# A spectral gating kernel on Trainium2: the last six lower-half filter products cut into column halves, and the work list written anew

## The chip, the cores and the metric

The kernel runs on one core of a Trainium2 chip. TensorE (PE) multiplies matrices, VectorE (DVE), ScalarE (ACT) and GpSimd (POOL) work element by element, SyncE (SP) only issues transfers; ACT and POOL issue transfers too. The engines run side by side, each through its own instructions in order, and wait for each other on semaphores. The metric is the device time of one execution in microseconds (us), the median over runs.

## The reference

```python
def _A_ref(x, w_r, w_i):                       # _B_ref is the same
    X = jnp.fft.rfft2(x.astype(jnp.float32), axes=(-2, -1))
    X = X * (w_r + 1j * w_i)
    return jnp.fft.irfft2(X, s=(S, D), axes=(-2, -1)).astype(jnp.bfloat16)

x = A_x                                        # (1, 2048, 1024) bf16
g = sigmoid((x * gate_w).sum(-1, keepdims=True))
return g * _A_ref(x, A_w_r, A_w_i) + (1 - g) * _B_ref(x, B_w_r, B_w_i)
```

Both branches work on the same x. It is transformed once, multiplied by two filters of 2048 x 513 complex numbers, and the two results are mixed row by row with the gate g. One inverse transform does for both, because the gate is folded into its row factors.

## The kernel before

**Stages.** The two-dimensional transform is done as matrix products with constant tables. A job name stands for one step on one piece of data:

- `load.x.g.dh`: one of 16 loads of x, 256 KB each: row group g (0 to 7), column half dh. `load.E`, `load.F2`, `load.CK` are tables. `egen` makes signed copies of E.
- `fold.g.k` and `s1m.g.j`, `s1e.g.j`: the first row transform. For a group in `FOLDED` (0, 1, 2 before) DVE makes the sum and the difference of columns d and 1023-d (two `tensor_tensor`, L456), and PE then needs 16 matmuls of 128 columns in a group. For the others DVE makes one reversed copy (L454), and PE does the fold itself with 16 matmuls of 256 columns. `s1e` takes the result out of PSUM.
- `s2m`, `s2e`: the column transform. `s4m`, `s4e`: the second row transform. Both run for p = 0 to 7 and for two column halves of the spectrum: h = 1 (upper) first, then h = 0 (lower).
- `swap.p.h` (two transfers within SBUF) and `xneg.p.h` (a sign) make the copy with real and imaginary parts exchanged.
- `prod.t.h`, t = 0 to 15: the filter products for both filters, one DVE `tensor_tensor` of 128x2048 at L317, both inputs in SBUF. Filters are loaded by `load.W.h.b.m.f`: h, the first block b of four t's, m blocks, filter f (A or B). Four slots hold them: three in tile WR, the fourth in tile FR. `wslot(h, b)` says which; a slot is loaded again only when the products that read it are done. `w5` takes a column of each upper block aside.
- `s5m.g`, `s5e.g`: the inverse second row transform; groups 16 to 31 read h = 1 products, groups 0 to 15 read h = 0 products. Every one of them waits for all 16 products of its half (key `("prod", h)`). `c0m`, `c0e` put the first column right.
- The gate: `gwm`, `gsm.t0.n` (dot products of x with gate_w taken from the transformed rows, n values of t at a time), `gse`, `rowsum`, `zsm`, `zse` (sigmoid), `zst` (store to a DRAM scratch tensor `zd`), `zld` (load it back, spread over the partitions, key `SI`). `stm`, `ste`, `stx`, `stp.k` serve the column 512.
- `rb.c` (POOL or DVE) multiplies a quarter of the inverse row table U5 with the gate, `al.c.k` rearranges it. `s6m`, `s6e`: the inverse first row transform. `s7m`, `s7c`, `s7p`, `fin`: the inverse column transform and its butterflies; `store.i.sg`: the output.

**Order.** The string `ORDER` (L21) lists all jobs. It is read once from left to right; each job appends its instructions to its engine's queue (the last letter of a job: a = ACT, d = DVE, p = POOL, s = SP), and the semaphore waits follow from the keys that the instructions read and write. So the list fixes the order on each engine, and it also fixes who gets which of the four PSUM units: `take` hands out the unit that was given back first. DVE works on the products while ACT takes `s5m` results of the upper half out of PSUM; SP issues the filter loads between them, one after another, and waits at each of them for its slot.

The lines that set when a product may start, and who waits for the products, are these:

```python
wslot = lambda h, b: b if h else b % 3                                   # L362
mult(Q[eng], o, i0, i1, r=K + KS + wkeys(slot, 0) + wkeys(slot, 1) + [("XN", t // 2, h)] + U * h, a=[("prod", h)])   # L544
r=["CK", ("prod", g // 16)] + (["col0"] if g == 0 else [])               # L670, s5m
mult(Q[eng], o, o, sl(F2, 512 * c, [(32, 16), (0, 2), (1, 32)]), r=["U5", "SI"], a=[("RP", c)])                      # L655, rb
```

Of the kernel before, what the change touches and what calls it, by code (L numbers as in the profile page):

```python
# [20 lines left out]
ORDER = """  # L21
load.E.1.s load.x.6.0.s zero load.SM.a load.GR.a egen.1.1 load.x.6.1.s egen.1.2 load.x.3.0.a load.x.0.0.s load.x.3.1.s egen.1.3 load.E.0.s
fold.6.0.d load.x.7.0.s load.x.7.1.s load.x.0.1.s warm.12x64x1.14x512x1 fold.3.0.d s1m.6.1 load.x.4.0.a s1e.6.1.d load.x.4.1.a s1m.6.0
s1m.3.1 fold.7.0.d load.x.1.1.s load.x.1.0.s egen.0.1 sig0 load.x.5.0.s rev s1e.3.1.a fold.0.1.d fold.0.0.d s1m.3.0 s1m.7.1 s1m.7.0
fold.4.0.d load.x.5.1.s s1e.3.0.a load.x.2.1.s s1m.0.0 s1e.7.1.a load.x.2.0.s s1e.6.0.a s1m.0.1 fold.1.1.d s1m.4.0 s1e.7.0.a s1m.4.1
fold.1.0.d s1e.0.1.a s1m.1.0 s1e.0.0.d s1e.4.0.a load.F2.s fold.5.0.d s1m.5.0 s1e.4.1.a s1m.5.1 load.CK.s load.W.1.0.3.1.s s1e.1.0.a
fold.2.0.d load.W.1.0.3.0.s fold.2.1.d s1m.2.1 s1e.5.0.a s1m.1.1 s1e.2.1.a s1e.5.1.d s1m.2.0 s1e.1.1.d s1e.2.0.a s2m.0.1 s2m.1.1 s2e.0.1.a
s2m.5.1 s4m.0.1 s2e.1.1.d s2e.5.1.d s4m.1.1 s2m.2.1 s4e.0.1.a s2m.4.1 s4e.1.1.a s2e.4.1.a s4m.5.1 s2e.2.1.d s2m.3.1 s2m.6.1 swap.0.1.p
s4e.5.1.a swap.1.1.p s2e.6.1.a s2e.3.1.d xneg.0.1.d w5.0.d s2m.7.1 s4m.3.1 s2e.7.1.a load.W.1.3.1.0.s prod.1.1.d swap.5.1.p xneg.1.1.d
s4m.4.1 s4m.2.1 s4m.6.1 prod.0.1.d prod.2.1.d prod.3.1.d s4e.3.1.a s4m.7.1 s4e.4.1.a s4e.2.1.a xneg.5.1.a swap.3.1.s prod.11.1.d swap.4.1.s  # L30
gwm gwe.a s2m.1.0 xneg.3.1.d gsm.12.4 w5.1.a s4e.7.1.a s4e.6.1.a load.VC.s swap.2.1.p gse.12.4.a w5.2.d load.W.1.3.1.1.s xneg.4.1.a gsm.0.4
s2e.1.0.a gse.0.4.a gsm.4.4 xneg.2.1.a swap.7.1.p s2m.0.0 gse.4.4.a s2m.2.0 s2e.0.0.a s2e.2.0.a s2m.5.0 gsm.8.4 prod.7.1.d s2e.5.0.a
prod.9.1.d prod.6.1.d gse.8.4.a prod.10.1.d s4m.1.0 s4m.0.0 s2m.7.0 s4e.1.0.a s2m.3.0 swap.6.1.p s4e.0.0.a xneg.7.1.a prod.8.1.d s2e.7.0.a
xneg.6.1.d prod.4.1.d prod.5.1.d load.W.0.0.1.0.s load.W.0.0.1.1.s s4m.2.0 swap.1.0.p rowsum.0.d prod.14.1.d prod.12.1.d s4e.2.0.a s2m.4.0
s2e.3.0.a s4m.5.0 s2m.6.0 swap.0.0.p stm load.W.0.1.2.1.s prod.15.1.d w5.3.a s4e.5.0.a prod.13.1.d rowsum.1.d load.W.0.1.2.0.s ste.a
xneg.0.0.a s5m.24 stp.2.d prod.0.0.d s4m.7.0 s2e.6.0.a swap.2.0.p s2e.4.0.a xneg.1.0.d swap.5.0.p s4m.3.0 s5e.24.a s4e.3.0.a s5m.19
s4e.7.0.a s5m.27 s5e.27.a rowsum.2.p swap.7.0.p prod.2.0.d s4m.4.0 s5m.29 swap.3.0.p s5m.16 s5e.19.a s4e.4.0.a prod.3.0.d prod.1.0.d s5m.23
xneg.5.0.d s5e.23.a stx.s s4m.6.0 zsm swap.4.0.s s5e.29.a s4e.6.0.a zse load.W.0.3.1.1.s s5m.22 xneg.2.0.d s5m.26 prod.11.0.d s5e.22.a
s5e.26.a prod.5.0.d zst.p s5e.16.a prod.4.0.d xneg.4.0.a load.W.0.3.1.0.s s5m.30 swap.6.0.p s5m.20 s5m.28 s5m.18 xneg.3.0.d s5e.30.a s5m.31
xneg.7.0.a prod.10.0.d s5e.28.a load.U5.s prod.7.0.d prod.6.0.d xneg.6.0.a prod.8.0.d s5m.21 s5e.18.a s5m.17 s5e.21.a s5e.31.a prod.9.0.d  # L40
prod.14.0.d prod.12.0.d s5e.20.a prod.13.0.d s5m.25 zld.s prod.15.0.d s5m.10 s5e.25.a s5m.6 s5m.12 s5e.17.d stp.0.d s5e.10.a s5m.9 s5m.11
s5e.6.d s5m.7 stp.1.d s5e.12.a rb.0.p s5m.8 rb.3.p s5e.9.a s5e.11.d s5e.7.a s5m.13 c0m s5e.8.d s5e.13.a s5m.4 c0e.d s5m.3 s5m.2 s5e.4.a
al.0.0.p s5e.3.d s5m.1 s5e.2.a s5m.14 s5m.5 s5e.1.d al.0.1.p s5e.14.a s5m.0 s5e.0.d rb.2.p s5m.15 rb.1.d s6m.0.1 al.1.1.d s5e.5.a s5e.15.a
s6e.0.1.a s6m.1.1 s6m.0.0 s6e.1.1.d s6e.0.0.a s6m.1.0 s6e.1.0.d al.2.1.p load.DI.s s7m.0 s7m.1 s7c.0.a s7p.0.0.d s7c.1.a s7p.0.1.d s7m.2
al.1.0.p s7p.1.0.d s6m.2.1 al.2.0.a s7c.2.a s6m.2.0 s7p.2.0.d s7p.2.1.d s6e.2.1.a s7p.1.1.d s6e.2.0.a s6m.3.0 fin.0.1.p fin.0.0.p s7m.3
fin.2.0.d s7c.3.a s6e.3.0.a s7m.4 fin.1.1.d s7c.4.a s6m.3.1 fin.1.0.d s7p.3.0.d s7p.3.1.d fin.2.1.p store.0.1.s s7m.5 s6e.3.1.a fin.3.0.p
s7p.4.0.d s6m.4.1 s7m.7 s7p.4.1.d s6m.4.0 fin.4.1.d s7c.5.a al.3.0.a fin.4.0.p s7p.5.0.d s7c.7.a s7p.5.1.d store.0.0.s fin.3.1.d s6m.5.1
al.3.1.a store.1.0.p s6e.4.1.a s7m.6 fin.5.0.d s6e.4.0.a s7p.7.0.d store.1.1.s s7p.7.1.d s7m.8 s7c.6.a s6m.5.0 fin.5.1.p fin.7.1.p s7p.6.0.d
s7c.8.a s7p.6.1.d s6e.5.1.a fin.7.0.d s7p.8.0.d store.5.1.s s6e.5.0.a fin.6.1.p store.4.1.s store.3.1.s s6m.6.1 store.5.0.s s7p.8.1.d
fin.6.0.d s7m.9 s6e.6.1.a s7m.10 store.6.0.s store.7.1.s fin.8.0.d store.3.0.p s7c.10.a s7m.11 s7c.9.a s6m.6.0 s7p.10.0.d s7c.11.a  # L50
store.2.1.a store.2.0.p s7p.10.1.d fin.8.1.p store.4.0.s s7p.9.0.d s7p.9.1.d fin.10.0.p s6m.7.1 fin.9.1.d store.7.0.s s6e.6.0.a s7p.11.0.d
store.8.0.p s6e.7.1.a s6m.7.0 s7p.11.1.d s6e.7.0.a s7m.13 fin.10.1.p s7c.13.a s7m.12 store.10.0.s fin.9.0.d store.8.1.p s7c.12.a store.9.0.s
s7m.14 s7p.13.0.d fin.11.1.p s7m.15 s7p.12.0.d fin.11.0.p s7c.14.a store.10.1.s s7p.13.1.d store.9.1.s s7p.12.1.d fin.13.1.p store.6.1.s
s7p.14.0.d store.11.0.s s7p.14.1.d s7c.15.a s7p.15.0.d store.14.0.a fin.13.0.p store.11.1.s store.14.1.a s7p.15.1.d store.13.1.a
store.15.0.s store.15.1.a fin.12.0.d fin.12.1.d store.12.1.a store.12.0.s store.13.0.p
# [329 lines left out]

# [426 lines left out]
```

## Time and profile before

| | us |
|---|---|
| three runs | 132.91, 132.07, 132.33 |
| median | 132.33 |
| the profiled execution, its own time | 132.75 |
| span of its instructions | 130.9 |
| busy: PE, DVE, ACT, POOL | 106.9, 104.2, 98.2, 51.0 |

The profiled execution took 1.85 us more than the span of its instructions, and it is 0.42 us above the median. Times in the views count from the start of the span. In a row of the timeline stand the start, the duration, engine, line, operation, written tile <- read tile, shapes and a count; rows of one kind that follow each other are merged, so a row with x9 is nine instructions. In brackets stands the idle time before it and what ended it. A row of the windows view has, for a stretch of time, the busy time and number of instructions of each engine, then the granted share of the TensorE clock, the busy share of the DMA engines, and GB/s.

### The profile page before, as it was taken

The page shows a single profiled execution, that of the slowest core. Times are in us where ns is not written, and L with a number is a line of the kernel's source. Part 1 is how long each engine was busy: PE and PEld are TensorE (multiplying, and loading weights), DVE is VectorE, ACT ScalarE, POOL GpSimd, SP SyncE. Part 2 cuts the span into 40 slices and gives each one's busy share as a digit, 9 for nine tenths or more (in the row PEclk, how much of TensorE's full clock was granted, in tenths as well). Part 3 has the DMA queues.
Part 4 walks back from the last instruction along what each step waited for, and adds up shares of the span by engine and source line. Part 5 has one row for each costly group of instructions (what it writes and reads, how often), then busy time and mean ns, then how long its engine had stood idle before and what let it go on. Part 6 is the DMA issues. An engine that isn't in the chain of part 4 may idle for free.

```text
span 130.9 us, 3622 instructions
## 1 busy us (share of the span) xinstructions
PE 106.9 (82%) x1522; PEld 88.5 (68%) x1529; DVE 104.2 (80%) x126; ACT 98.2 (75%) x120; POOL 51.0 (39%) x63
## 2 busy tenths in 40 slices
PE   6966789699999999778775358999999997969920
PEld 3344577588759988546475258999999896959500
DVE  0404795373699998999499999988699999999990
ACT  1913599647799969999999994899568987766410
POOL 3000000007316106332540007990439394949970
...
GB/s 108 253 279 371 348 385 304 201 264 323 290 115 224 292 148 189 252 297 326 267 162 214 250 403 233 5 0 5 0 5 40 80 23 88 103 276 43 203 200 241
DMA packets 27314, 25.55 MB, mean 195 GB/s; under 512 B 2706, under 2 KB 23458, under 8 KB 27042
## 3 DMA queue, kind: packets, MB, share of 16 engines
...
## 4 chain that ended last, share of the span: by engine, by line
PE 50%; ACT 19%; DVE 13%; DMA 6%; issue 5%; SPq 3%; DVEq 1%
PE PS L332 50%; ACT FR L312 9%; ACT WP L312 7%; DMA WP<-in_A_x_dram 6%; DVE FR L729 4%; DVE WP L317 4%; SPq L308 3%; ACT FR L321 2%; DVE WR L735 2%; DVE FR L314 2%; DVEq L751 1%; DVE WR L729 1%; DVE WP L314 0%; ACT XST L312 0%; ACT W L312 0%
## 5 line engine op out<-in xcount | busy, mean ns | idle before, releaser
L312 ACT ACTIVATE WP<-PS 128x1024 bf16<-128x1024 f32 x51 | 50.2, 1035 | 11.9 <-PE PS L332 11.7
L312 ACT ACTIVATE FR<-PS 128x1024 bf16<-128x1024 f32 (+1 forms) x44 | 36.6, 897 | 11.9 <-PE PS L332 11.9
L332 PE MATMUL PS<-FR,WP 128*128 128x128 bf16 (+2 forms) x383 | 32.9, 245 | 2.2 <-DVE FR L729 1.9
L332 PEld LDWEIGHTS PS<-FR,WP 128*128 128x128 bf16 x384 | 28.5, 130 | 6.2 <-DVE FR L729 2.8
L332 PE MATMUL PS<-CK,WP 128*128 128x64 bf16 x512 | 22.5, 209 | 8.5 <-ACT WP L312 4.9
L332 PEld LDWEIGHTS PS<-CK,WP 128*128 128x128 bf16 x512 | 20.9, 121 | 10.5 <-ACT WP L312 5.8
L735 POOL TENSOR_TENSOR WR<-FR 128x512 bf16<-128x512 f32 x15 | 20.3, 1379 | 9.9 <-DVE FR L729 9.8
L314 DVE CAST WP<-PS 128x1024 bf16<-128x1024 f32 (+1 forms) x14 | 16.1, 1166 | 7.3 <-PE PS L332 7.3
L317 DVE TENSOR_TENSOR WP<-FR,WR 128x2048 bf16<-128x2048 bf16 x16 | 18.5, 1220 | 1.8 <-issue 1.8
L332 PE MATMUL PS<-F,FR 128*128 128x128 bf16 x256 | 17.3, 230 | 1.3 <-DVE FR L314 1.3
L308 POOL DMA_DIRECT2D WP<-WP x12 | 6.7, 558 | 29.5 <-ACT WP L312 29.5
L332 PEld LDWEIGHTS PS<-F,FR 128*128 128x128 bf16 x256 | 16.2, 104 | 2.7 <-DVE FR L314 1.4
L729 DVE TENSOR_TENSOR FR<-PS,FR 128x512 f32<-128x512 f32 x28 | 17.5, 679 | 0.4 <-ACT FR L312 0.4
L332 PE MATMUL PS<-WP 128*128 128x256 bf16 (+1 forms) x128 | 12.7, 253 | 3.9 <-DMA WP<-in_A_x_dram 1.8
L332 PEld LDWEIGHTS PS<-WP 128*128 128x128 bf16 x128 | 10.3, 98 | 6.5 <-DMA WP<-in_A_x_dram 2.1
L317 DVE TENSOR_TENSOR WP<-WP,WR 128x2048 bf16<-128x2048 bf16 x12 | 14.0, 1221 | 0.0
L308 POOL DMA_DIRECT2D FR<-FR x14 | 7.9, 569 | 13.8 <-PE PS L332 12.9
L735 DVE TENSOR_TENSOR WR<-FR 128x512 bf16<-128x512 f32 x13 | 12.7, 1010 | 0.1
L317 POOL TENSOR_TENSOR FR<-FR,F 128x1024 bf16<-128x1024 bf16 x3 | 6.4, 2144 | 10.4 <-DMA F<-zd 10.4
L332 PE MATMUL PS<-WP,CK 128*128 128x512 bf16 (+4 forms) x42 | 7.8, 324 | 0.1
L314 DVE COPY WP<-WP 128x1024 bf16<-128x1024 bf16 x5 | 2.1, 423 | 7.2 <-DMA WP<-in_A_x_dram 7.2
L332 PE MATMUL PS<-FR,CK 128*128 128x512 bf16 (+1 forms) x32 | 7.0, 352 | 1.0 <-ACT FR L312 0.8
(51 smaller groups left out, 79.1 us busy)
## 6 DMA issues: line engine op xcount, KB each, us to landing
WP<-in_A_x_dram SPq DMA_DIRECT2D x13, 256.0 KB, 7.8
out_dram<-WR SPq DMA_DIRECT2D x20, 128.0 KB, 2.1
FR<-FR POOLq DMA_DIRECT2D x14, 128.0 KB, 3.1
WP<-WP POOLq DMA_DIRECT2D x12, 128.0 KB, 3.4
...
WP<-in_A_x_dram ACTq DMA_DIRECT2D x3, 256.0 KB, 7.8
out_dram<-WR POOLq DMA_DIRECT2D x6, 128.0 KB, 2.2
```

Source lines behind the costliest of these rows:

```text
L308: return P.add(eng, lambda e: e.dma_start(dst, src), dma=name, **kw)
L312: P.add("act", lambda e: e.activation(dst, src, ACT.Copy), **kw)
L314: P.add(eng, lambda e: e.tensor_copy(dst, src), **kw)
L317: P.add(eng, lambda e: e.tensor_tensor(out=dst, in0=s0, in1=s1, op=ALU.mult), **kw)
L321: P.add("act", lambda e: e.activation(dst, src, ACT.Copy, scale=SM[:, col:col + 1]), **kw)
L332: P.add("pe", lambda e: e.matmul(o, lh, rh, start=first, stop=last), **kw)
L729: P.add(Q[eng], lambda e: e.tensor_tensor(out=o, in0=ps(u * 1024, [(1, 512)]), in1=eos(i), op=ALU.subtract if s else ALU.add), r=[("EO", i ...
L735: P.add(Q[eng], lambda e: e.tensor_tensor(out=od, in0=pv[0], in1=pv[1], op=ALU.subtract if s else ALU.add), r=[("PQ", i % NPQ, 0), ("PQ", ...
L751: with nc.Block() as block:
```

## The change

- `FOLDED` becomes (0, 1, 2, 3): group 3 is folded on DVE as well.
- `HALVED = (5, 6, 7)`: the lower-half products of p = 5, 6, 7 (t = 10 to 15) become two instructions each, for the lower and the upper 32 of 64 column blocks (`prod.t.0.0`, `prod.t.0.1`, 128x1024 each). The key of the lower half is split likewise: `s5m` groups 0 to 7 wait for part 0, groups 8 to 15 for part 1. `s4e` of these p's writes another layout.
- `wslot(1, b)` becomes `(b - 1) % 4`: upper blocks 1, 2, 3 lie in WR and are loaded first, block 0 lies in FR.
- `gsm` runs in eight groups of two t's instead of four groups of four.
- `keep.k.n` is new: n matmuls of 512 columns whose result nobody reads. `keep.3.2` stands ahead of `s2m.3.0`, `keep.1.2` ahead of `s5m.7`, `keep.2.2` and `keep.0.2` behind the last `s7m`.
- The list is new. On the engines' queues: five more loads of x go by ACT and five fewer by SP; three `xneg` and one `s4e` move from ACT to DVE, one `s5e` from DVE to ACT, `rb.1` from DVE to POOL; `c0e` goes to ACT; `stp.1` stands ahead of the lower products with t = 10 and up and `stp.0` between their first and their second halves. `w5` is all on ACT, and one `s1e` and one `s6e` more are on DVE; `al` has two jobs on POOL (four before), four on ACT (three), two on DVE (one); SP issues one swap more and three stores fewer. The upper products run in the order 10 11 4 7 6 5 15 8 1 9 3 0 14 12 13 2, before 1 0 2 3 11 7 9 6 10 8 4 5 14 12 15 13.

```diff
-FOLDED = (0, 1, 2)
+FOLDED = (0, 1, 2, 3)
+HALVED = (5, 6, 7)
...
-    wslot = lambda h, b: b if h else b % 3
+    wslot = lambda h, b: (b - 1) % 4 if h else b % 3
...
+    def keep(k, n):
+        u = take("keep", k)
+        for v in range(n):
+            mm(ps(u * 1024 + 512 * (v % 2), [(1, 512)]), sl(CK, 0, [(1, 128)]), sl(CK, 0, [(1, 512)]), True, True, r=["CK"], w=banks(u)[v % 2:v % 2 + 1])
+        give("keep", k)
...
-    def prod(t, h, eng):
+    def prod(t, h, c, eng):
...
+        nq, q0 = (64, 0) if c == 2 else (32, 32 * c)
...
+        mult(Q[eng], o, i0, i1, r=K + KS + wkeys(slot, 0) + wkeys(slot, 1) + [("XN", t // 2, h)] + U * h,
+             a=[("prod", h, v) for v in range(2) if c in (2, v)])
...
-               r=["CK", ("prod", g // 16)] + (["col0"] if g == 0 else []), w=banks(u)[q // 8:q // 8 + 1])
+               r=["CK", ("prod", g // 16, g % 16 // 8)] + (["col0"] if g == 0 else []), w=banks(u)[q // 8:q // 8 + 1])
```

The part of the two lists that the prediction follows, one engine each, from the end of the upper products on:

```
DVE before  prod.13.1 rowsum.1 stp.2 prod.0.0 xneg.1.0 prod.2.0 prod.3.0 prod.1.0 xneg.5.0 xneg.2.0 prod.11.0 prod.5.0
            prod.4.0 xneg.3.0 prod.10.0 prod.7.0 prod.6.0 prod.8.0 prod.9.0 prod.14.0 prod.12.0 prod.13.0 prod.15.0
            s5e.17 stp.0 s5e.6 stp.1 s5e.11 s5e.8 c0e s5e.3 s5e.1 s5e.0 rb.1 al.1.1 s6e.1.1 s6e.1.0 s7p.0.0
DVE after   prod.13.1 rowsum.0 prod.2.1 rowsum.1 xneg.0.0 xneg.1.0 prod.0.0 xneg.5.0 prod.2.0 prod.3.0 stp.2 stp.1 prod.1.0
            xneg.2.0 prod.11.0.0 prod.4.0 xneg.4.0 prod.10.0.0 prod.5.0 prod.8.0 prod.9.0 xneg.7.0 prod.6.0 prod.15.0.0
            prod.7.0 prod.14.0.0 prod.13.0.0 prod.12.0.0 stp.0 prod.13.0.1 prod.11.0.1 prod.10.0.1 prod.12.0.1 prod.14.0.1
            prod.15.0.1 s5e.0 s5e.2 s5e.5 s5e.11 s5e.10 s5e.14 s6e.0.1 al.2.0 al.1.0 s6e.1.1 s6e.1.0 s7p.0.0
SP before   load.W.1.0.3.0 load.W.1.3.1.0 swap.3.1 swap.4.1 load.VC load.W.1.3.1.1 load.W.0.0.1.0 load.W.0.0.1.1
            load.W.0.1.2.1 load.W.0.1.2.0 stx swap.4.0 load.W.0.3.1.1 load.W.0.3.1.0 load.U5 zld load.DI
SP after    load.W.1.1.3.0 load.W.1.0.1.0 swap.7.1 load.W.1.0.1.1 swap.6.1 load.VC load.W.0.0.1.1 load.W.0.0.1.0 swap.5.0
            load.W.0.1.2.1 load.W.0.1.2.0 swap.3.0 stx load.W.0.3.1.0 load.W.0.3.1.1 load.U5 zld load.DI
POOL before zst swap.6.0 rb.0 rb.3 al.0.0 al.0.1 rb.2 al.2.1 al.1.0 fin ...
POOL after  swap.4.0 swap.6.0 swap.2.0 rowsum.2 swap.7.0 zst rb.0 al.0.0 al.0.1 rb.2 rb.1 rb.3 fin ...
PE after    ... s5m.19 keep.1.2 s5m.7 c0m s5m.3 s5m.0 s5m.6 s5m.2 s5m.1 | s5m.15 s5m.9 s5m.5 s5m.13 s5m.11 s5m.4 s5m.10
            s5m.14 s5m.12 s5m.8 s6m.0.1 s6m.1.1 s6m.0.0 s6m.1.0 s7m.0
```

More of the change, by code (lines that the diff above doesn't have):

```diff
@@ L25 @@
[L25 to L48, printed above, removed]
@@ new lines @@
+prod.12.1.2.d s2e.6.0.a swap.5.0.s s4e.4.0.a s4m.2.0 s4m.6.0 keep.3.2 prod.13.1.2.d s2m.3.0 w5.0.a load.W.0.1.2.1.s rowsum.0.d s4e.2.0.a
+prod.2.1.2.d rowsum.1.d stm s4e.6.0.a ste.a s4m.7.0 s5m.23 xneg.0.0.d s5m.26 s2e.3.0.a s4m.3.0 s4e.7.0.a xneg.1.0.d prod.0.0.2.d s5e.26.a
+s5m.21 load.W.0.1.2.0.s xneg.5.0.d prod.2.0.2.d s5m.28 prod.3.0.2.d s4e.3.0.a s5m.16 s5e.23.a s5e.28.a s5m.18 swap.4.0.p s5m.22 s5e.18.a
+swap.6.0.p swap.2.0.p s5m.30 rowsum.2.p s5e.16.a s5m.24 swap.3.0.s stp.2.d s5e.21.a stp.1.d prod.1.0.2.d s5m.17 xneg.6.0.a xneg.2.0.d
@@ new lines @@
+prod.11.0.0.d prod.4.0.2.d s5e.22.a stx.s xneg.4.0.d load.W.0.3.1.0.s prod.10.0.0.d prod.5.0.2.d prod.8.0.2.d swap.7.0.p s5e.17.a zsm
+prod.9.0.2.d s5m.25 load.W.0.3.1.1.s zse s5e.24.a xneg.3.0.a s5e.30.a zst.p s5m.31 s5e.31.a xneg.7.0.d s5m.29 prod.6.0.2.d prod.15.0.0.d
+prod.7.0.2.d s5e.29.a s5e.25.a prod.14.0.0.d prod.13.0.0.d prod.12.0.0.d s5m.20 stp.0.d prod.13.0.1.d s5m.27 s5e.27.a s5m.19 s5e.20.a
+keep.1.2 s5m.7 c0m prod.11.0.1.d prod.10.0.1.d s5e.19.a load.U5.s s5m.3 c0e.a s5e.7.a s5e.3.a zld.s prod.12.0.1.d prod.14.0.1.d
```

58 lines of the change are left out of this document (40 added, 18 removed).

## The prediction

> **What bounds it now.** I read the windows by stage first, then the chain of waits in order of time, then the timelines of DVE, POOL and SP around its turns. The windows give, for each stretch, the busy time of PE, PEld, DVE, ACT and POOL, the granted PE clock, the DMA share and GB/s:
>
> ```profile
> 0.00:24.60 24.60, 18.15 (x154) 12.65 (x155) 11.70 (x18) 15.27 (x16) 1.41 (x7) 1.00 0.94 291
> 35.20:56.40 21.20, 19.39 (x297) 15.63 (x298) 20.79 (x24) 19.90 (x30) 7.14 (x14) 0.92 0.68 204
> 56.40:79.10 22.70, 15.01 (x271) 11.72 (x273) 20.84 (x23) 22.58 (x27) 4.87 (x9) 0.88 0.90 280
> 79.10:94.30 15.20, 15.06 (x336) 14.93 (x336) 13.11 (x14) 11.85 (x12) 10.58 (x7) 0.84 0.09 37
> 94.30:126.60 32.30, 28.81 (x319) 24.48 (x320) 31.75 (x45) 22.15 (x31) 23.14 (x21) 1.00 0.27 100
> 43.00:46.50 3.50, 3.44 (x35) 3.18 (x33) 3.50 (x4) 3.42 (x6) 0.00 (x0) 0.52 0.90 271
> 79.00:84.50 5.50, 5.37 (x106) 5.38 (x107) 5.50 (x6) 3.09 (x4) 5.16 (x3) 0.54 0.24 101
> ```
>
> The load stage is bound by transfers (DMA share 0.94). From 35.2 to 79.1 DVE is busy 41.6 of 43.9 us and sets the end of the products. From 79.1 PE starts the whole inverse of the lower half at once, at first at half clock (0.54), and is busy 15.06 of 15.20. The last stage is DVE's again, 31.75 of 32.30. The chain says the same where the stages meet:
>
> ```profile
> 74.45 4.63 DVE WP L317 x4
> 79.13 14.10 PE PS L332 x320
> ```
>
> The four last products release 320 matmuls; until the last product is done none of lower groups 0 to 15 can start. That turn, 79.07 to the first s7p, is what the halves are to shorten: with them groups 0 to 7 start before the last six half products. DVE shows the prices:
>
> ```profile
> 14.54 1.29 DVE L456 TENSOR_TENSOR WP<-WP 128x1024 bf16<-128x1024 bf16 x2
> 35.15 0.49 DVE L323 TENSOR_SCALAR WP<-WP,SM 128x1024 bf16<-128x1024 bf16 x1 [1.15 <-DMA WP<-WP]
> 35.55 0.17 DVE L314 COPY W<-WR 128x16 bf16<-128x16 bf16 x1
> 50.62 0.68 DVE L317 TENSOR_TENSOR WP<-WP,GSB 128x512 f32<-128x512 bf16 x1
> 56.26 0.68 DVE L601 TENSOR_REDUCE AT<-WP 128x32 f32<-128x512 f32 x1
> 64.96 3.50 DVE L317 TENSOR_TENSOR WP<-FR,WR 128x2048 bf16<-128x2048 bf16 x3 [1.80 <-issue]
> 68.77 10.30 DVE L317 TENSOR_TENSOR WP<-FR,WR 128x2048 bf16<-128x2048 bf16 x9
> 78.99 1.22 DVE L314 CAST WP<-PS 128x1024 bf16<-128x1024 f32 x1
> 80.12 1.42 DVE L317 TENSOR_TENSOR PST<-XST,W 128x64 bf16<-128x64 bf16 x1
> 82.60 1.05 DVE L317 TENSOR_TENSOR PST<-XST,W 128x64 bf16<-128x64 bf16 x1
> 90.89 0.68 DVE L317 TENSOR_TENSOR FR<-FR,F 128x1024 bf16<-128x1024 bf16 x1
> 95.60 1.29 DVE L729 TENSOR_TENSOR FR<-PS,FR 128x512 f32<-128x512 f32 x2 [0.15 <-ACT FR L312]
> ```
>
> Neighbours overlap a little, so I price by intervals: a whole product (10.30 - 1.22)/8 = 1.135; a half, of a fold's shape, 1.29 - .68 = .61; xneg 35.55 - 35.15 = .40; rowsums .62 and .60; a cast of s5e 1.14. The stall of 1.80 before 64.96 is prod.11.0 waiting for load.W.0.1.2, issued by SP from 51.75 on. And POOL, beside it:
>
> ```profile
> 79.34 4.25 POOL L317 TENSOR_TENSOR FR<-FR,F 128x1024 bf16<-128x1024 bf16 x2 [10.38 <-DMA F<-zd]
> 83.56 1.50 POOL L329 TENSOR_SCALAR FR<-FR 128x512 bf16<-128x512 bf16 x1
> 85.02 0.60 POOL L314 COPY FR<-FR 128x512 bf16<-128x512 bf16 x1
> 85.60 2.13 POOL L317 TENSOR_TENSOR FR<-FR,F 128x1024 bf16<-128x1024 bf16 x1
> ```
>
> rb.0 and rb.3 (2.13 each) start when the gate has landed (F<-zd), by luck just behind the last product. The tiny stp.0 and stp.1 (128x64, two SBUF inputs) took 1.42 and 1.05: they ended where rb.0 (79.34 + 2.13 = 81.47) and rb.3 (83.59) ended. The casts out of PSUM between them kept 1.22. So a DVE operation with two SBUF inputs waits for the POOL operation in flight, and POOL for it; they take turns. This decides the forecast.
>
> **The change, part by part.** *Load stage.* Fold of group 3: DVE two adds (1.21) for one copy, PE less; five x loads go by ACT. The bytes stay and DMA is at 0.94, so 0; bounds -.4 (a step of a load's arrival) to +1.2 (fold late behind its load). *Gate.* Eight gsm groups hold the same 128 matmuls; DVE's gapless chain covers PE there (20.79 of 21.20). Spreading them should spare the fall to 0.52 at 43.0, worth up to half of 3.5 = 1.7 us of PE, hidden; without that cover it is gained. *keep.* 8 matmuls of 512 columns, in PE's idle time (22.70 - 15.01 in the second product stage) or behind s7m: 0, at most one PSUM turn of .9 us. ACT loses three xneg and its stage keeps its slack to DVE: 0. *Product chain.* DVE now issues 11 xneg, 26 whole products, 12 halves, the rowsums and three stp (.17 each, like the small copy): 11 x .40 + 26 x 1.135 + 12 x .61 + 1.22 + .51 = 42.96, so 35.15 + 42.96 = 78.1 with no wait; before, 79.07 with 2.2 of waits. Up to prod.11.0.0 it is 9 xneg, 20 products, rowsums, two stp: 27.9, so DVE is ready for it at 63.05.
>
> *SP, which it then waits for.* The twelve W.0.0.1 issues, the eight of W.0.1.2, stx, a swap, the eight of W.0.3.1, U5, zld:
>
> ```profile
> 29.04 1.95 PE L332 MATMUL PS<-F,FR 128*128 128x128 bf16 x32
> 31.69 2.84 PE L332 MATMUL PS<-F,FR 128*128 128x128 bf16 x48
> 46.71 0.94 PE L332 MATMUL PS<-GW,FR 128*128 128x2 bf16 x32
> 42.34 1.09 ACT FR L312
> 43.28 0.60 SPq L308 DMA_DIRECT2D WR<-in_A_w_r_dram  x1
> 51.75 0.63 SPq L308 DMA_DIRECT2D WR<-in_B_w_r_dram  x1
> 58.48 2.76 SPq L308 DMA_DIRECT2D XST<-XST  x2
> 63.91 1.10 SPq L308 DMA_DIRECT2D FR<-FR  x2
> 65.11 0.65 SPq L308 DMA_DIRECT2D WR<-in_B_w_r_dram  x1
> 71.70 0.60 SPq L308 DMA_DIRECT2D FR<-c_U  x1
> 72.40 2.65 SPq L308 DMA_DIRECT2D F<-zd  x4
> WR<-in_A_w_i_dram SPq DMA_DIRECT2D x2, 256.0 KB, 7.2
> F<-zd SPq DMA_DIRECT2D x4, 128.0 KB, 4.8
> ```
>
> swap.6.1 now stands ahead of load.VC and W.0.0.1, and needs the s4 result of p = 6, upper half. PE has 18 groups of s2 and s4 to do for it from 24.6 on, .89 each (48 matmuls took 2.84, 32 took 1.95), and four gsm groups of .47: 42.5, with some .2 of narrow matmuls 42.7; an ACT turn of 1.09 (a piece of the chain): 43.8. From one issue to the next a swap takes 65.11 - 63.91 = 1.2 and a constant like VC .6 to .7: W.0.0.1 starts at 45.7 (before 43.28), lasts 51.75 - 43.28 = 8.4 to 54.1; swap.5.0 1.1 to 1.2; W.0.1.2 starts at 55.2 instead of 51.75. Its slots are free by then: the last reader is prod.13.1, at about 54.2. Landing: before, prod.11.0 started 13.2 after the first issue, which gives 68.4; the seventh issue at +6.1 plus 4.8, the shortest time to landing here, gives 66.1. I take 67.3, the middle, since neither queue is clearly shorter: a stall of 4.2 instead of 1.8. Behind it: 6 halves, 6 products, 2 xneg, stp.0 = 11.4, so part 0 is complete at 78.7, and the six second halves would end at 82.3.
>
> *The meeting with POOL.* SP goes on: 55.2 + 6.7 (58.48 - 51.75) + swap.3.0 1.1 + stx 2.8 + W.0.3.1 6.6 (71.70 - 65.11) = 72.4 for U5, zld 73.1 to 75.75; before, rb.0 began 4.3 behind the end of zld's issues (79.34 - 75.05), so rb.0 begins at 80.0 (bounds 79.3, as before, and 81.5). Three halves are done by 80.5; then they take turns: rb.0 to 82.65, half 83.25, al.0.0 to 84.75, half 85.35, al.0.1 to 85.95, half 86.55. That is 82.3 + 4.25; bounds 0 (rb.0 later than the last half) and 10 (all six halves meet rb.0, al, rb.2, rb.1, rb.3 in turn). The last product ends at 86.55, 7.5 later than before.
>
> The Trainium skill (SBUF — State Buffer, "Who interferes with whom") says that a DVE instruction with two SBUF inputs contends with a GpSimd instruction that reads SBUF, and that the second fully waits. The 1.42 and 1.05 of stp agree with it; were it otherwise, the turn would cost 0 and the forecast would be 130.5.
>
> *The turn.* Groups 0 to 7 are through PE by 83 (8 x .53), so behind 86.55 DVE has six casts 6.84, three s6e 3.42, two al of .3, and some .65 of gaps: 11.5 to the first s7p instead of 95.60 - 79.07 = 16.5. So s7p.0.0 comes at 86.55 + 11.5 = 98.05: **+2.45**. Eight groups in 4.46 us show that PE is no limit here at full clock:
>
> ```profile
> 85.78 4.46 PE L332 MATMUL PS<-CK,WP 128*128 128x64 bf16 x128
> ```
>
> c0e on ACT and rb.1 on POOL (2.13 instead of DVE's .68) stand off this path: rb.1 ends near 91. *Last stage.* DVE's and POOL's fins stay 13 and 15: 0, bounds -1.5 and +1.5 for the turns that they too take. Sum: 0 + 2.45. The profiled execution took 132.75 and lies .42 above the median of 132.33; 135.2 against it is **134.8** against the median.
>
> **Rivals.** (1) *The gate comes behind the last half*, the other side. If W.0.1.2 lands by 65.0, as it did before, the last half ends at 79.9, ahead of rb.0 at 80.0; s7p.0.0 at 79.9 + 11.5 = 91.4, -4.2: 128.1 (with no filter wait at all 126.2). With the late filter but a gate later than 82.3 it is 93.8, -1.8: 130.5. It is decided by rb.0's start against the last half's end. For it: the queues before had room at 58 to 63, and the swaps ahead have moved to POOL. Against: W.0.1.2 starts 3.45 later by SP's row, and what delays the filter delays the gate only through the same SP queue. (2) *One or two halves meet POOL*, an excess of 2.15 to 3.65: -0.5 to +1.9 around 132.5. That is the case in which the change gains its turn and gives it back. (3) *The filter is later still*, 68.4 or more, or the gate as early as 79.3: five or six halves meet POOL, excess 8.5 to 10: 82.3 + 9 + 11.5 = 102.8, +7: 139 to 141. (4) *The clock falls.* Slices with idle PE were followed by 0.54 in 79.0 to 84.5; while the halves wait, PE idles from 83 to 86.5. Eight groups would cost .81 for .53 each, 2.2 more of PE, of which DVE's casts hide about one: 136 to 137. The Trainium skill (TensorE: Matmul & The Clock Gate) has the clock fall after about one idle window of 3.4 us; the 0.54 agrees, and 3.5 us of idleness stands right at that edge.
>
> **How the numbers follow.** Chances: the forecast 36% (its own range 133.7 to 136.5), rival 1 28%, rival 2 16%, rival 3 13%, rival 4 7%. The bounds of rb.0 (79.3 to 81.5) and of the filter (65 to 68.4) move the gap of 2.3 us between rb.0 and the last half by about as much as it is wide, so more than a quarter falls to rival 1. The range leaves out half of rival 1's early end and most of rival 3: 128.5 to 139.5. A measurement of this kernel can tell about 1% from no change (131.0 to 133.65): faster is rival 1 (.28) and a little of 2, together .30; same .16; slower .54.
>
> **What would show it.** Right: DVE idle for about 4 us ahead of prod.11.0.0 until 67; rb.0 at 80 with second halves that last 2 us instead of .68; granted clock near 1 in the lower s5m; no dip at 43; s7p.0.0 near 98 and 32 us behind it unchanged. Wrong: a filter that has landed by 65, halves that keep .68 beside rb.0, or an rb.0 that starts behind them; then the time is rival 1's.

## The result: 4 per cent slower

| | before | changed |
|---|---|---|
| executions, us | 131.8 to 132.9 | 137.85, 137.89, 141.16, 141.95 |
| median, us | 132.2 | 139.5 |
| ratio, 95% interval | | 1.042 (1.035 to 1.050) |
| forecast, us | | 134.8 (128.5 to 139.5) |

The ratio leaves disturbed executions out and so is nearer to 138 than to the median. The profiled execution of the result is the one of 141.2. A repeated run of the same kernel gave a profile of an execution of 138.0 (span 135.8, against 130.9 before), and that one is read first. Its windows, with columns as in the prediction, cut where the stages meet (the first xneg, the last gate product, the last half product, the first s7p):

```profile
35.65:57.50 21.85, 20.19 (x311) 15.33 (x313) 21.72 (x25) 21.40 (x36) 6.08 (x12) 1.00 0.59 176
57.50:87.00 29.50, 18.02 (x359) 15.61 (x359) 21.72 (x32) 22.74 (x29) 8.20 (x10) 0.83 0.81 247
87.00:100.10 13.10, 12.83 (x284) 12.36 (x281) 11.86 (x13) 10.71 (x14) 10.43 (x6) 1.00 0.01 3
100.10:132.90 32.80, 28.53 (x308) 24.23 (x307) 31.48 (x46) 20.57 (x29) 24.34 (x21) 0.95 0.30 110
```

The upper products are DVE's as before (21.72 of 21.85). The turn behind the last half is 13.1 us where it was 16.5, and the last stage is nearly the same length. The loss is in the second row: from 57.5 to 87.0 DVE is busy only 21.72 of 29.50. DVE's timeline shows where:

```profile
65.70 0.48 DVE L326 TENSOR_SCALAR FR<-FR,SM 128x1024 bf16<-128x1024 bf16 x1 [0.61 <-DMA FR<-FR]
71.19 1.83 DVE L320 TENSOR_TENSOR WP<-FR,WR 128x1024 bf16<-128x1024 bf16 x2 [5.00 <-DMA WR<-in_A_w_i_dram]
...
79.67 3.63 DVE L320 TENSOR_TENSOR WP<-FR,WR 128x1024 bf16<-128x1024 bf16 x5 [0.71 <-DMA WR<-in_B_w_i_dram]
83.22 0.19 DVE L320 TENSOR_TENSOR PST<-XST,W 128x64 bf16<-128x64 bf16 x1
83.32 3.70 DVE L320 TENSOR_TENSOR WP<-FR,WR 128x1024 bf16<-128x1024 bf16 x6
...
100.07 2.47 DVE L746 TENSOR_TENSOR FR<-PS,FR 128x512 f32<-128x512 f32 x4
```

prod.11.0.0 waits 5.00 us for the filter W.0.1.2 and starts at 71.19, 6.2 us later than prod.11.0 before. The six second halves, 83.32 to 87.02, run back to back at .6 each: they pay nothing for POOL, though POOL's rb.0 came in their midst.

```profile
83.50 5.53 POOL L320 TENSOR_TENSOR FR<-FR,F 128x1024 bf16<-128x1024 bf16 x1 [12.73 <-DMA F<-zd]
89.12 1.50 POOL L332 TENSOR_SCALAR FR<-FR 128x512 bf16<-128x512 bf16 x1
```

rb.0 is drawn out from 2.13 to 5.53 and ends 2.0 us behind the last half. In the turn behind it DVE waits .99 and .25 for PE. Its two al take 1.55 (.49 in d2 below, where POOL is done by then): the first stands until POOL's last rb ends, at 91.17 + 6.36 = 97.53.

```profile
90.28 4.65 DVE L317 CAST WP<-PS 128x1024 bf16<-128x1024 f32 x4 [0.99 <-PE PS L335]
95.18 1.23 DVE L317 CAST WP<-PS 128x1024 bf16<-128x1024 f32 x1 [0.25 <-PE PS L335]
96.33 1.55 DVE L332 TENSOR_SCALAR FR<-FR 128x512 bf16<-128x512 bf16 x2
```
```profile
91.17 6.36 POOL L320 TENSOR_TENSOR FR<-FR,F 128x1024 bf16<-128x1024 bf16 x3
```

SP's queue shows why the filter is late:

```profile
45.42 1.13 SPq L311 DMA_DIRECT2D WP<-WP  x2
46.64 0.54 SPq L311 DMA_DIRECT2D WP<-c_V  x1
47.28 1.20 SPq L311 DMA_DIRECT2D WR<-in_B_w_r_dram  x1
...
55.88 1.18 SPq L311 DMA_DIRECT2D FR<-FR  x2
57.10 0.65 SPq L311 DMA_DIRECT2D WR<-in_B_w_r_dram  x1
```

SP stands at swap.6.1 until 45.42, then come VC, W.0.0.1 (47.28), swap.5.0 and W.0.1.2 at 57.10, against 51.75 before. prod.11.0.0 starts 14.1 us behind that first issue (before: 13.2).

The 141.2 us of the result's own profile come from two more things, each seen in it alone of these two. In 24 to 31 us, the s2m stage, the clock was granted at half; the first row is that profile's, the second the repeat's:

```profile
24.00:31.00 7.00, 5.88 (x59) 5.62 (x57) 2.66 (x3) 2.86 (x3) 0.00 (x0) 0.51 0.96 261
```
```profile
24.00:31.00 7.00, 5.81 (x88) 4.99 (x87) 5.01 (x5) 3.29 (x5) 0.00 (x0) 1.00 1.17 290
```

59 matmuls instead of 88 in the same time: everything behind starts 2.3 us later (the first xneg at 37.94, not 35.65). Just ahead, in 20.4 to 23.8, PE had been busy 1.45 of 3.4 us (3.28 in the repeat). That alone doesn't explain the fall: from 9.4 to 12.8 PE was busy only .83 of 3.4 us in the same profile, and the clock stayed at 1.00 behind it. The Trainium skill (TensorE: Matmul & The Clock Gate, "What's actually happening") has the clock fall after about one idle window, some 3.4 us; here it fell though PE was idle for only 1.95 us of such a stretch. And in that profile rb.0 came a little ahead of stp.0 and held it (DVE's row, then POOL's):

```profile
85.33 2.16 DVE L320 TENSOR_TENSOR PST<-XST,W 128x64 bf16<-128x64 bf16 x1
```
```profile
85.30 2.13 POOL L320 TENSOR_TENSOR FR<-FR,F 128x1024 bf16<-128x1024 bf16 x1 [10.64 <-DMA F<-zd]
87.53 4.92 POOL L332 TENSOR_SCALAR FR<-FR 128x512 bf16<-128x512 bf16 x1
```

### The profile page after: what moved, and what is told of

Its sections match the earlier page's. It is cut to its first block, busy times and chain, and to the rows that moved or that the text cites. A ratio compares the mean times of both kernels' runs of the same rounds, so it can differ in the third digit from the quotient of the medians.

```text
span 139.0 us, 3668 instructions
## 1 busy us (share of the span) xinstructions
PE 111.5 (80%) x1537; PEld 90.4 (65%) x1537; DVE 108.2 (78%) x135; ACT 93.2 (67%) x122; POOL 54.4 (39%) x60
## 4 chain that ended last, share of the span: by engine, by line
PE 43%; DMA 18%; DVE 15%; ACT 15%; issue 4%; SPq 2%; DVEq 0%; POOL 0%
PE PS L335 43%; DMA WP<-in_A_x_dram 11%; ACT FR L315 6%; ACT WP L315 6%; DVE WP L320 6%; DMA FR<-FR 4%; DMA WP<-WP 3%; DVE FR L746 2%; DVE WP L465 2%; SPq L311 2%; DVE PST L320 1%; DVE WR L746 1%; DVE WR L752 1%; ACT FR L324 1%; ACT WP L324 1%
## 5 line engine op out<-in xcount | busy, mean ns | idle before, releaser
L315 ACT ACTIVATE WP<-PS 128x1024 bf16<-128x1024 f32 (+1 forms) x51 | 48.9, 1018 | 19.6 <-PE PS L335 19.6
L317 DVE CAST WP<-PS 128x1024 bf16<-128x1024 f32 x14 | 16.7, 1220 | 8.0 <-PE PS L335 8.0
L320 DVE TENSOR_TENSOR WP<-FR,WR 128x1024 bf16<-128x1024 bf16 (+1 forms) x22 | 19.2, 930 | 3.9 <-DMA WR<-in_A_w_i_dram 3.9
L335 PE MATMUL PS<-F,FR 128*128 128x128 bf16 x256 | 18.8, 239 | 1.1 <-ACT FR L315 1.1
L335 PEld LDWEIGHTS PS<-F,FR 128*128 128x128 bf16 x256 | 17.6, 109 | 2.8 <-ACT FR L315 1.4
L335 PE MATMUL PS<-WP 128*128 128x128 bf16 (+1 forms) x128 | 12.4, 253 | 5.1 <-DVE WP L465 3.5
L752 DVE TENSOR_TENSOR WR<-FR 128x512 bf16<-128x512 f32 x13 | 13.4, 1050 | 0.0
L320 POOL TENSOR_TENSOR FR<-FR,F 128x1024 bf16<-128x1024 bf16 x4 | 8.5, 2136 | 10.6 <-DMA F<-zd 10.6
L311 POOL DMA_DIRECT2D FR<-FR x12 | 6.7, 560 | 14.4 <-PE PS L335 13.8
L335 PE MATMUL PS<-FR,CK 128*128 128x512 bf16 (+1 forms) x36 | 8.8, 382 | 0.4 <-ACT GSB L315 0.4
L465 DVE TENSOR_TENSOR WP<-WP 128x1024 bf16<-128x1024 bf16 x8 | 5.1, 687 | 4.2 <-DMA WP<-in_A_x_dram 4.2
```

The lines of the kernel that those rows point to most:

```text
L311: return P.add(eng, lambda e: e.dma_start(dst, src), dma=name, **kw)
L315: P.add("act", lambda e: e.activation(dst, src, ACT.Copy), **kw)
L317: P.add(eng, lambda e: e.tensor_copy(dst, src), **kw)
L320: P.add(eng, lambda e: e.tensor_tensor(out=dst, in0=s0, in1=s1, op=ALU.mult), **kw)
L335: P.add("pe", lambda e: e.matmul(o, lh, rh, start=first, stop=last), **kw)
L465: P.add(Q[eng], lambda e: e.tensor_tensor(out=fs, in0=xs(0, 1), in1=xs(511, -1), op=ALU.subtract if k else ALU.add), **kw)
```

## The experiments

The theory to test, from these rows, is A: what the time pays is the wait for W.0.1.2. Its rivals are B, the load stage; C, the meeting of rb and half products that the forecast had priced; and D, the clock behind PE's idle time. The labels (c1 and so on) are used in the expectations too. Ratios are to the kernel before, run on the same chip.

**The changed kernel again (a1_again).** No edit.

> The changed kernel once more, unchanged. All theories: about 1.04 times the kernel before (138 us). What it tells: the profiled execution of the result took 141.2 us, two other executions 137.9. If the load stage is what differs (theory B below), an execution near 138 has s2m starting at 26 as before but the granted clock at 1 in 24 to 31 us, or s2m starting by 25; if the wait for load.W.0.1.2 differs (theory A), prod.11.0.0 starts well before 74.1 with the same load stage.

Ratio 1.041 (1.031 to 1.052). Its profile is the one above: the s2m stage ran at full clock, so the clock has a part in the spread, and the filter's wait was there all the same. The load stage did not run at full clock in it: PE was granted half from 12 to 18 us, and s2m began at 26.1 (26.2 in the profile of the result).

**swap.6.1 off SP's queue (a2_swap6_pool).**

```diff
-swap.6.1.s prod.9.1.2.d s4e.0.0.a
+swap.6.1.p prod.9.1.2.d s4e.0.0.a
```

> Only swap.6.1 is moved, from SP's queue to POOL's, which is idle there. In the changed kernel SP stood still from 45.87 to 47.70 for it, and with its own issues and VC behind it W.0.0.1 began at 50.51. Theory A (SP's order delays the filter W.0.1.2, and the wait of 3.9 + 2.5 us before prod.11.0.0 is what the time pays): W.0.0.1 starts 2 to 3 us earlier, W.0.1.2 lands 2 to 3 us earlier, and the time falls by 2 to 3 us to about 135.5. Theory B (the load stage and its clock are what the time pays): no change, 138. Theory C (POOL's rb.0 against the half products): no gain either, since rb.0 moves with the same queue; within 1 us of 138.

Ratio 1.026 (1.018 to 1.034). W.0.0.1 started at 44.07 (47.28), W.0.1.2 at 55.28 (57.10), prod.11.0.0 at 69.52 (71.19), the first s7p at 97.58 (100.07). One swap in the wrong queue is worth about 2 us, as A has it. W.0.1.2 gained less than W.0.0.1: ahead of it on SP stands swap.5.0, which could be issued only at 54.11, when ACT was done with s4e.5.0, and its slots wait for prod.13.1, done at 55.06.

**Two x loads earlier on ACT (a3_x30_early).**

```diff
-load.x.7.0.a s1m.1.1 load.GR.a fold.5.0.d
+load.x.7.0.a s1m.1.1 load.x.7.1.a load.x.3.0.a load.GR.a fold.5.0.d
...
-load.x.7.1.a s1m.2.1 s1m.5.0 s1e.2.0.a s1m.1.0 load.x.3.0.a s1e.2.1.d
+s1m.2.1 s1m.5.0 s1e.2.0.a s1m.1.0 s1e.2.1.d
```

> Only load.x.7.1 and load.x.3.0 are moved on ACT, ahead of load.GR and thus ahead of the s1e that they waited behind (x.3.0 was issued at 11.18 and landed at 20.55, behind F2 and CK). Theory B: the last x lands by 19, s2m starts 1.5 to 2 us earlier than 26.2, PE's idle stretches of 20 to 26 us shrink, the granted clock stays at 1 in 24 to 31, and the time falls by 2 to 4 us to 134 to 136. Theory A: SP's filter loads start earlier only as far as s4e.6.1 does, so at most the same 1.5 to 2 us. Theory C: nothing, 138.

Ratio 1.023 (1.013 to 1.033), resting on two executions (135.5 and 136.3): about 2 us. In its profile, of an execution of 137.6, s2m started at 24.71 instead of 26.1, and W.0.1.2 at 56.45. Not all of the earlier s2m is the loads': the clock was 1.00 through this load stage, and half from 12 to 18 us in the repeat. Whether the gain adds to the swap's is asked with c3.

**Whole products (a4_whole_products).** HALVED = (), each product at the place of its first half.

> The halves undone: HALVED is empty and the six products are whole, each at the place of its first half. The result of all three theories that the halves themselves gain: the last product ends near 88.6 (85.4 + 6 x .53) and not at 91.1, but all 16 lower groups wait for it, and with the turn of 16.5 us of the kernel before the first s7p comes near 105, against 103.7: 1 to 2 us slower than the changed kernel, 139 to 140. If the halves cost by meeting POOL (theory C), it is 1 to 3 us faster, 135 to 137.

Ratio 1.067 (1.060 to 1.074). The last product ended at 86.24, stp.0 then lost 2.15 to rb.0, and the first s7p came at 104.09, 4.0 us behind the repeat's (1 to 2 were expected): the turn took 17.85 with whole products, 13.05 with halves. In the new list the halves gain about 3.5 us, and all else loses about 9.

**The halves alone (b1_halves_only).** The kernel before, with its list, slots and folds, and the six halves; from the last first half on the lower groups as in the changed kernel.

```diff
-prod.15.0.d s5m.10 s5e.25.a s5m.6 s5m.12 s5e.17.d stp.0.d
+prod.15.0.0.d s5e.25.a s5e.17.d stp.0.d stp.1.d s5m.7 c0m s5m.3 c0e.a s5e.7.a s5e.3.a
+prod.13.0.1.d prod.11.0.1.d prod.10.0.1.d prod.12.0.1.d prod.14.0.1.d prod.15.0.1.d s5m.0
...
```

> The kernel before with the halves alone: its own list, slots, folds and gsm groups up to the last first half, then the changed kernel's order of the lower groups (0 to 7 first, stp and c0m ahead of the second halves, c0e on ACT). Theory A (the halves gain about 4 us, as the run with whole products showed, and the new list's late filters lose about 9): part 0 complete near 76, last half near 79.5 or a little later for stp, first s7p near 92 to 93 instead of 95.6, the time 2 to 3.5 us below the kernel before: 129 to 131. Rival (the halves only gain where the filter is late and PE waits): no gain, since ACT takes upper groups out of PSUM until 79 anyway: 132 to 133.

Ratio 1.007 (1.002 to 1.012): the rival was right. DVE's timeline at the end of the products:

```profile
75.25 2.50 DVE L321 TENSOR_TENSOR WP<-FR,WR 128x1024 bf16<-128x1024 bf16 x4 [1.44 <-DMA WR<-in_A_w_i_dram]
77.67 1.22 DVE L318 CAST WP<-PS 128x1024 bf16<-128x1024 f32 x1
78.81 0.28 DVE L321 TENSOR_TENSOR PST<-XST,W 128x64 bf16<-128x64 bf16 x2
79.01 3.70 DVE L321 TENSOR_TENSOR WP<-FR,WR 128x1024 bf16<-128x1024 bf16 x6
...
89.62 1.90 DVE L321 TENSOR_TENSOR FR<-FR,F 128x1024 bf16<-128x1024 bf16 x1
```

Part 0 is complete at 77.75 instead of 79.07 for the whole, for the next filter block is late by 1.44; the last half ends at 82.71, and DVE's rb.1 then takes 1.90 beside POOL instead of .68. The turn fell from 16.5 to 14.3, the last product came 3.6 later. The halves gain nothing by themselves.

**Filters early (c1_filters_early).** Both edits above, swap.5.0 on POOL too, stp.0 behind prod.6.0, xneg.6.1 on DVE, and the upper products with t = 9, 14, 12, 13 sooner:

```diff
-prod.15.1 prod.8.1 prod.1.1 prod.9.1 prod.3.1 prod.0.1 prod.14.1 prod.12.1 prod.13.1 prod.2.1
+prod.15.1 prod.8.1 prod.9.1 prod.14.1 prod.1.1 xneg.6.1.d prod.12.1 prod.13.1 prod.3.1 prod.0.1 prod.2.1
```

> The changed kernel with x.7.1 and x.3.0 early on ACT, swap.6.1 and swap.5.0 on POOL, stp.0 ahead of the last first halves, xneg.6.1 on DVE and the upper products of t = 9, 14, 12, 13 ahead of 3, 0, 2, so that prod.13.1, for which W.0.1.2's slots wait, is done near 52.9 instead of 55.1. Theory A (the landing of W.0.1.2, 14 us behind its first issue in every run, sets the time): it starts near 53.3, lands near 67.5, prod.11.0.0 starts there, against 69.5 with swap.6.1 alone and 71.2 without; first s7p near 95.5, the time 133 to 134. Rival: the landing is bound by the bytes in flight and not by its start; then prod.11.0.0 stays at 69 to 70 and the time at 135.5.

Ratio 1.008 (1.003 to 1.013). Most of the loss is gone, and what c1 has beyond c3 below (1.024) is there only to issue W.0.1.2 earlier. That speaks for A: the filter's way is most of what the kernel paid for. Its profile can't show the step by itself, for it is of the longest of the ten executions (134.94, median 133.29). In it W.0.1.2, issued from 54.32 on, landed only for 69.31, 15.0 us later, where the rival had it; the time is where A had it. d1 asks why the landing takes so long.

**PE kept busy ahead of the lower groups (c2_keep16).**

```diff
-keep.1.2 s5m.7 c0m
+keep.1.16 s5m.7 c0m
```

> The changed kernel with keep.1.16 in place of keep.1.2: 16 matmuls without a reader ahead of s5m.7, about 3.4 us at full clock, in the 5 to 6 us in which PE waits for the first halves. Theory D (the turn behind the last half took 13 us and not 11.5 because the clock had fallen to half while PE idled): the granted clock in the lower s5m rises from .5 to near 1 and the first s7p comes 1 to 2 us earlier: 136 to 137. Rival (the turn is bound by ACT and DVE, which take the groups out of PSUM): the clock rises and the time stays at 138.

Ratio 1.034 (1.023 to 1.046). The windows of ten us from about 1 us after s5m.7's start, for this run and for the repeat:

```profile
86.00:96.00 10.00, 9.70 (x265) 9.41 (x262) 9.56 (x11) 9.11 (x11) 9.90 (x5) 1.00 0.17 66
```
```profile
84.00:94.00 10.00, 9.86 (x265) 9.70 (x263) 9.01 (x12) 8.30 (x10) 9.90 (x5) 0.87 0.17 70
```

The clock rose to 1.00 and the same 265 matmuls ran: last half 88.72, first s7p 101.74, a turn of 13.0 as in the repeat (100.07 - 87.02 = 13.05); both times are 1.7 later there, since this profile's s2m stage ran at half clock. A higher clock alone does not shorten the turn, so D falls as told. DVE waited less for PE (.44 and .22), but its two al then took 2.15, up to the end of POOL's last rb at 99.20. The time doesn't decide: 1.034 is no different from the repeat's 1.041 within the intervals.

**Swap and loads together (c3_three_moves).** The edits of a2 and a3, and stp.0 behind prod.6.0.

> The changed kernel with swap.6.1 on POOL, x.7.1 and x.3.0 early on ACT, and stp.0 behind prod.6.0 instead of behind the last first half, so that rb.0 can't come ahead of it. If the filter and the load stage add up: the gain of the swap alone (2.3 us) and of the loads alone (1 to 2.4 us) overlap where both make s4e.6.1 earlier, so 134 to 135.5. POOL: by what two runs showed (rb.0 drawn out to 5.5 us, the half products undisturbed), stp.0 takes .2, the second halves .68 each, and rb.0 ends only 2 us behind the last half. If instead they take turns, some halves last 2 us and the time is 2 to 4 us higher.

Ratio 1.024 (1.015 to 1.032), no better than the swap alone. W.0.1.2 started at 55.34 (55.28 there). In both SP comes to it from swap.5.0, which had to wait for s4e.5.0 and was issued at 54.17 (54.11 there); prod.13.1 was done at 54.49 here, so it was no longer what SP waited for. The two gains are one: they make s4e.6.1 earlier, and the next wait in line takes the rest. stp.0 took .18, the halves .69, and rb.0 5.1.

**Two swaps later (d1_swaps_late).** On c1, by engine (POOL, then DVE):

```diff
-swap.4.0.p swap.6.0.p swap.2.0.p rowsum.2.p swap.7.0.p zst.p
+swap.2.0.p swap.4.0.p rowsum.2.p zst.p swap.7.0.p swap.6.0.p
...
-prod.13.0.0.d prod.12.0.0.d
+xneg.6.0.d prod.13.0.0.d prod.12.0.0.d
```

xneg.7.0 moves too, on DVE, from ahead of prod.6.0 to behind stp.0.

> The kernel with the early filters (c1), with two swaps of the lower half, 6.0 and 7.0, moved on POOL behind zst, so that they no longer move data while W.0.1.2 is on its way, swap.4.0 behind swap.2.0, and xneg.6.0 on DVE. Theory E (W.0.1.2 lands late because five swaps share the transfer engines with it, about .75 us each, where the kernel before had three): prod.11.0.0 starts at 67.5 to 68 instead of 69.3, and the time falls by 1 to 1.5 us, from 133.3 to about 132, level with the kernel before. Rival (the landing is bound by the filter's own rows): prod.11.0.0 stays at 69.3 and the time at 133.3, or rises by .4 for the xneg.

Ratio 1.063 (1.057 to 1.068), and yet prod.11.0.0 started at 66.18 instead of 69.31. From W.0.1.2's first issue to that start it took 13.4 instead of 15.0, with two swaps fewer in the stretch. The other profiles of the new list say the same: 14.0 to 15.0 in the nine without this move, 12.9 to 13.4 in the five with it. So the expectation's theory E holds, at about .6 a swap (means of 14.4 and 13.1). The other 1.5 us are an earlier first issue (52.81), which this edit needn't have brought, since c1's profile was of its longest execution. The time was lost behind it. DVE's row of two first and six second halves, and POOL's:

```profile
78.60 11.54 DVE L321 TENSOR_TENSOR WP<-FR,WR 128x1024 bf16<-128x1024 bf16 x8
```
```profile
79.47 2.42 POOL L321 TENSOR_TENSOR FR<-FR,F 128x1024 bf16<-128x1024 bf16 x1 [8.04 <-DMA F<-zd]
81.99 1.81 POOL L333 TENSOR_SCALAR FR<-FR 128x512 bf16<-128x512 bf16 x1
83.76 0.78 POOL L318 COPY FR<-FR 128x512 bf16<-128x512 bf16 x1
84.51 7.63 POOL L321 TENSOR_TENSOR FR<-FR,F 128x1024 bf16<-128x1024 bf16 x3
```

Eight halves took 11.54 instead of 4.9, each POOL operation .2 to .4 more than alone: here they do take turns, and five of the six second halves wait for one. This is the third rival of the forecast, met in another kernel.

**The same with s5m.5 ahead of s5m.15 and s5m.9 (d2_swaps_late_s5m5).**

> The same with s5m.5 ahead of s5m.15 and s5m.9, so that DVE has a group to take out of PSUM where it stood still for 1.1 to 1.2 us before s5e.5 in every run of the new list. If the turn behind the last half is bound by DVE's casts, the first s7p comes 1 us earlier than in d1; if it is bound by PE's groups and the four PSUM units (ten groups behind the last half, then 4 x .98 of s6m), less than .5 us.

Executions from 134.2 to 143.0, too far apart for a ratio, so what s5m.5 is worth stays open. In the profiled one (134.2) three of the six second halves waited (2.64, 1.09 and 1.10 instead of .69), and the last ended at 84.57.

**rb behind the last half, in three kernels (f3_d1_rb_waits on d1, f1_d2_rb_waits on d2, f2_after_rb_waits on the changed kernel).** One edit:

```diff
-r=["U5", "SI"], a=[("RP", c)]
+r=["U5", "SI", ("prod", 0, 1)], a=[("RP", c)]
```

> The kernel with two swaps late (d1, 140.7 us, its second halves lasting 2.6, 1.1, .7, 1.1, 2.6 and 2.6 us beside rb and al) with one edit: rb also waits for the last half product. Theory F (all of d1's time above the kernel with early filters comes from half products and POOL operations taking turns): every second half lasts .69, the last ends near 83.5 instead of 90.1, rb.0 starts there, first s7p near 96 instead of 103.5, the time falls by 6 to 8 us to 133 to 134. Rival (d1 lost by its late swap.6.0 and the wait of 1.6 us for it, and the turns only fill time that was idle anyway): 138 to 140.

> The same edit on the kernel d2, whose executions spread from 134.2 to 143.0. Theory F: no spread of more than 2 us, last half near 82, first s7p near 94 to 95.5, the time 131 to 133, level with the kernel before or below it. Rival (rb now starts too late and the s6m wait for it): first s7p 96.5 or later, 134.

> The same edit on the changed kernel alone. In the run repeated (138.0) rb.0 was held up until the last half anyway, in the profiled execution of the result (141.2) rb.0 came first and stp.0 lost 2.1. Theory F: at most those 2 us in some of the executions, so 137.5 to 138, with less spread; the loss against the kernel before stays about 4 per cent, since it is the filter's. If the collision were what the changed kernel pays (the recorded forecast), 133 to 134.

On d1 the ratio fell from 1.063 to 1.015 (1.008 to 1.021), and the same eight halves took 4.91:

```profile
78.43 4.91 DVE L321 TENSOR_TENSOR WP<-FR,WR 128x1024 bf16<-128x1024 bf16 x8
```

On d2 the spread went from 8.8 to 2.0 us, ratio 1.025 (1.020 to 1.030); the first s7p came at 98.28, later than expected, behind waits of 1.66 and .54 for the late swaps and .64 for the last filter block, W.0.3.1. On the changed kernel: 1.042 (1.037 to 1.047), as without the edit. So C is real, but the half products of the changed kernel don't pay for it.

**The late swaps on SP behind the last filter (g1_swaps_on_sp).** On f1, by engine (SP, then POOL):

```diff
-load.W.0.3.1.1.s load.U5.s
+load.W.0.3.1.1.s swap.7.0.s swap.6.0.s load.U5.s
...
-zst.p swap.7.0.p swap.6.0.p
+zst.p
```

> The kernel f1 (early filters, late swaps, rb behind the last half) with swap.7.0 and swap.6.0 on SP behind the last filter load instead of on POOL behind zst: they no longer share the engines with W.0.1.2, and they don't wait for the gate. If the three costs found so far are the whole loss (filter late, POOL in turns, x.7 and x.6 late in f1: 1.66 + .64 + .54 us of waits), prod.11.0.0 starts near 66, part 0 is complete near 78, the last half ends near 81.7 with no second half above .7, first s7p near 94.5, and the time is 131 to 132, at or just below the kernel before. Rival (SP's later U5 and gate, 2.4 us, now hold up rb and so s6m): first s7p 96 or later, 133 to 134.

Every step came out as expected but the last: ratio 1.0045 (1.001 to 1.008), 133.3 us beside 132.85. DVE's rows:

```profile
65.78 1.83 DVE L321 TENSOR_TENSOR WP<-FR,WR 128x1024 bf16<-128x1024 bf16 x2 [1.84 <-DMA WR<-in_A_w_i_dram]
...
76.54 4.91 DVE L321 TENSOR_TENSOR WP<-FR,WR 128x1024 bf16<-128x1024 bf16 x8
...
94.89 2.49 DVE L747 TENSOR_TENSOR FR<-PS,FR 128x512 f32<-128x512 f32 x4
```

The filter's wait is 1.84 again, as it was before the change (1.80), no half is held, and the first s7p is at 94.89 (95.60 before); this profile is of the shortest of its twelve executions (132.01). So the loss can be undone with the halves kept. g1 holds all the moves of c1 and d2 and the edit of rb, and what each is worth by itself is known only as far as the runs above take it alone. None of the kernels run beats the one before.

## Why the prediction was wrong

The direction was right; the size was not, and the sum came near some of its marks by errors that cancelled. That the last half came within .5 of its mark is luck: what stands ahead of it was 4.6 late, and the 4.25 put down for the meeting with POOL were not paid. Its steps against the repeat:

| step | forecast | repeat | off |
|---|---|---|---|
| first xneg | 35.15 | 35.65 | +.5 |
| W.0.1.2, first issue | 55.2 | 57.10 | +1.9 |
| prod.11.0.0 | 67.3 | 71.19 | +3.9 |
| part 0 complete | 78.7 | 83.30 | +4.6 |
| last half product | 86.55 | 87.02 | +.5 |
| first s7p | 98.05 | 100.07 | +2.0 |

- **The filter (the term that was mis-sized).** The forecast saw that swap.6.1 now stands ahead of W.0.0.1 on SP and that prod.11.0.0 would stall; it gave 2.35 us (67.3 against 64.96), and 6.2 were measured. 1.6 of the difference is s4e.6.1, done at 45.39 instead of 43.8, since s2m began at 26.1 and not at 24.6. The load stage, which I had set to 0, cost these 1.5: x.3.0 waits on ACT behind an s1e (a3), and the clock was at half from 12 to 18 us; the runs don't part the two. 2.0 is the landing, 14.1 us behind the first issue where I took the middle of my bounds, 12.1. 1.1 of this is the step down from the 13.2 of the kernel before. (The lower bound was misread: the seventh issue stood at 56.55, +4.8 and not +6.1, which would have put the middle lower still.) The other .9 lies beyond even the upper bound. I had not counted that the swaps on POOL move their data while this filter does; two fewer in the stretch make the landing about 1.3 shorter (d1). Before, five swaps ran in that stretch too, but three of them only in its last 3.5 us. DVE itself was ready at 66.18 and not at 63.05, since two xneg waited 1.42 and .61 for their swaps; behind the filter that cost nothing.
- **The last filter block.** I let part 0 follow by DVE's work alone; prod.15.0.0 waited another .71 for W.0.3.1, which sits behind it on SP.
- **The meeting with POOL.** The step that failed outright: "Three halves are done by 80.5; then they take turns", +4.25. In the repeat it cost the halves 0, and making rb wait gained nothing (f2). The case that decides it, rb.0 coming while DVE issues halves back to back, was not in the trace of before: there the casts stood between stp.0 and stp.1. The mechanism exists and can cost 6 us (d1 against f3), but as told it decided nothing here. In the repeat DVE and POOL met later, at al, where the forecast had no term. The Trainium skill (SBUF — State Buffer, "Who interferes with whom") says that who issues first blocks the other: the 2.16 of stp.0 agrees with that; six halves that pass a waiting rb.0 go beyond it.
- **The turn.** 11.5 forecast, 13.05 measured. The casts of s5e and s6e took about what was put down for them. The two al took 1.55 and not .6, since the first met POOL's last rb, and DVE waited 1.24 for PE where .65 of gaps were put down. I had groups 0 to 7 through PE by 83; none had started, for part 0 was complete only at 83.30. At the end of the last half PE was in its fourth group, and ten more stand in the list behind the halves. Full clock alone didn't shorten the turn (c2).
- **Clock.** Rival 4 had the fall in the lower s5m; it was there (.87 over ten us) and cost nothing that c2 could get back. That "the 0.54 agrees" with an idle window says too much: in the trace of before the clock had already fallen between 72.5 and 75.5 (.72 in the mean), when PE's gaps had been 1.2 us. Where it cost 2.3 us, in the s2m stage of the profiled execution, the text had only a bound of 1.2 for the load stage.
- **Right:** the halves shorten the turn (13.05 against 17.85 with whole products, a4); the last stage is unchanged (first s7p to the last fin 32.8, before 32.2); the dip of the clock at 43 is gone; the case for "faster" needed the filter by 65, and when g1 brought it at 65.8 the first s7p came at 94.89, near the 95.60 before and not at rival 1's 91.4.

The range ended at 139.5, by the case of a filter at 68.4 and five or six halves in turns. The measured 1.042 times 132.33, 137.9, lies inside it, but by another way: up to the first s7p the filter came 3.9 later than forecast, the last block added .7 and the turn 1.55, and the 4.25 of the turns fell away.
